# A long convolution by two-stage DFT: the second stage and its inverse as 32x32 products, and the exchanged rows from TensorE in place of DMA copies

## The chip, the cores and the metric

The kernel runs on one NeuronCore of a Trainium2 chip. The metric is device time in microseconds (us) of one execution, the median over several runs. A profile of one execution is at hand beside it. Engine names are those of the profile: PE is TensorE (PEld its weight loads), DVE is VectorE, ACT is ScalarE, POOL is GpSimd and SP is SyncE, which here only issues DMAs.

## The reference, cut to what matters

Two branches start from the same normalized input and meet at the end. Branch A is a long convolution (sequence 2048, 640 channels), done in the reference by an FFT of length 4096. Branch B is a feed-forward block with 1728 hidden units.

```python
xn = layernorm(A_q)                                   # 2048 x 640
k_shift = 4-tap causal filter of A_k with A_shift_k
kv = k_shift * A_v
y = irfft(rfft(kv, 4096) * rfft(A_ssm_k, 4096))[:2048] + kv * A_ssm_D
s = xn * y
h = gelu(xn @ B_w1 + B_b1)                            # 2048 x 1728
g = silu(h @ B_w2 + B_b2)                             # 2048 x 640
out = A_q + s * g
```

## The kernel before, in words

**The convolution.** The sequence index is split as 16 p + n, with p on the 128 partitions and n from 0 to 15. The first DFT stage is, for each n, two 128x128 products (cosine and sine matrices `WA`, `WB`), each on 640 columns in two halves of 320: `k_f1` (steps kf) for the filter, `u_f1` (uf) for the signal. Their results go through DRAM scratch (`scrK`, `scrU`) and come back with rows regrouped, so that one group g (there are 32) has on its 128 partitions 4 blocks of 32 rows: 16 values of n times real and imaginary part. The second stage is a 16-point complex DFT inside each block of 32 rows. Before the change it is one product with the 128x128 matrix `F2m`, which is zero outside its four diagonal 32x32 blocks (the mask in `small_phase`, lines 285 to 288, makes these zeros): `k_f2` (ff, line 480) for the filter, whose 32 results are kept in `Khat`, and `u_f2` (mu, line 521) for the signal. Both call `mm2` (line 335), which makes two matmuls of 128x128 by 320 columns.

**Product and inverse.** Real and imaginary parts stand on even and odd partitions, so the complex product needs the filter's rows once as they are and once with neighbours exchanged. `swap_load` (mk, line 515) fetches the exchanged rows of two groups with two DMAs on the SP queue, from `Khat` to a ring of eight slots behind it (`NR`). `product` (mp, line 523) is one VectorE instruction per group: the PSUM tile `mu` (128 x 640, f32) is read twice, times the plain and the exchanged rows, into `p` (2 x 640 columns, bf16). `inv1` (mc, line 530) is the inverse of the second stage: for each half of the columns a product with `I1a` on the first part of p and one with `I1b` on the second, accumulated in PSUM; `inv1_out` (me) evacuates it on ScalarE (three times on VectorE), and `c_store` writes it to DRAM scratch `scrC`, from which the last stage (`inv2`, steps y) reads.

**The feed-forward block** runs through the same TensorE queue: `ffn1` (h: 5 matmuls of 512 columns), its GELU on ScalarE, `ffn2` (g: 14 matmuls of 320 columns), SiLU and products.

**Order of the work.** It is written out by hand: `PLAN` is a list of step names, issued in this order; every engine runs its own instructions in the order of the list. In PLAN, a letter behind a dot says which engine evacuates (a: ScalarE, d: VectorE).

**PSUM.** The steps ff, uf, kf, mu, mc, y and some transposes take their tile from one pool, `ps_big`, of three buffers of two banks each, in turn. A step that takes a buffer waits until the tile taken three places before has been read: a mu tile by its mp, an mc tile by its me, an ff tile by its fe. A stretch of PLAN before the change:

```
mu3 mp3 mk5 ml12 h30 he30 ml11 mc2 me2.a mu4 mp4 mc1 me1.a ms0 mu5 mp5 mk6 h31 he31 ml6 ff20 fe20.a mc3 me3.a
ms1 ln15 mu6 mp6 mc4 me4.a mu7 mp7 mk7 ml9 h32 he32 mu8 mp8 mc5 me5.a ms2 mc6 me6.a mu11 mp11 mc7 me7.a ms3 mu10
```

Of the kernel before, what the change touches and what calls it, by code (L numbers as in the profile page):

```python
# [35 lines left out]
te9.a kt4 gm5 kf7 cv26 cv27 cv28 kf6 kc4.a ke6.a ke7.a ks3 g6 ge6 kf8 ke8.a kf9 ke9.d ks4 kf10 ke10.a K2 tt8
te8.a kt6 kc6.d kf11 ke11.a ks5 kt9 kc9.d gm3 kf12 ke12.a tt5 te5.d tt6 te6.a uf1 kt7 kf13 kc7.a ke13.a ks6 g7
ge7 ls12 uf0 ue0.a ue1.d us0 cv29 cv30 cv31 V3 h14 he14 kf14 ke14.d kf15 ke15.d ks7 h15 he15 kt8 kc8.d kf19 kf18
ke18.a ke19.d ks9 kt10 kc10.a cv32 cv33 cv34 cv35 cv36 kf16 ke16.a kt12 cv40 kf17 kc12.a ke17.a ks8 h16 he16 uf3
uf2 ue2.a ue3.a us1 h17 he17 kf21 kf20 ke20.a ke21.d ks10 kt11 kc11.a h18 he18 uf5 uf4 ue4.a ue5.d us2 kf22  # L40
ke22.d ls10 h19 he19 kt14 kf24 ke24.d sm kf23 kc14.a ke23.a ks11 h20 he20 kf25 ke25.d ks12 kt13 kc13.d kf28
ke28.a h21 he21 uf6 ue6.a kf29 ke29.a ks14 uf7 ue7.a us3 h22 he22 h23 he23 kf26 ke26.a gm7 cv37 cv38 cv41 cv42
cv39 kf27 ke27.a ks13 kt15 kc15.d kf30 ke30.a kf31 ke31.a ks15 fl0 fl1 fl2 h24 he24 fl4 uf10 ue10.a gm6 ls15 ls8
ls9 uf8 ue8.a ls14 uf11 ue11.a us5 h25 he25 h26 he26 uf14 ue14.a cv43 ls13 lv3 lr3 h27 he27 cv44 ls11 lv2 lr2
cv45 cv46 cv47 uf12 ue12.a uf9 ue9.a us4 fl3 uf15 ue15.a us7 g8 ge8 gm8 ln13 ln9 uf13 ue13.a us6 fl5 g9 ge9 ff3
fe3.a ln12 ff1 fe1.d ln10 ff2 fe2.a cv56 ff0 fe0.a cv48 cv49 cv50 ln8 uf21 uf20 ue20.a ue21.a us10 ff8 fe8.a
ln11 g10 ge10 uf16 ue16.a ff6 fe6.d gm9 ff9 fe9.a fl7 ff5 fe5.a ff7 fe7.a fl9 ff4 fe4.a fl8 uf17 ue17.a us8 g11
ge11 cv51 cv52 cv53 cv54 cv55 ff11 fe11.a ff10 fe10.a fl6 uf18 ue18.d uf19 ue19.a us9 fl11 uf26 ue26.a cv57 cv58
cv59 uf24 ue24.a uf27 ue27.a us13 uf25 ue25.a us12 fl12 ff16 fe16.d ff17 fe17.a fl15 ff12 fe12.a tt12 te12.a
ff14 fe14.a cv60 cv61 cv62 cv63 ff18 fe18.a ff15 fe15.a fl13 g12 ff19 fe19.a fl10 uf22 ue22.d ff13 fe13.a fl14  # L50
uf31 gm11 ge12 uf30 ue30.a ue31.d us15 ff23 fe23.d gm12 uf23 ue23.a us11 gm10 tt14 te14.d uf29 uf28 ue28.d
ue29.a us14 mk0 ml0 ml1 mk1 mk2 mk3 ml2 ml3 ml5 ml4 ff31 fe31.a tt13 te13.a tt10 te10.d it0 ie0.d ff27 fe27.d
ff25 fe25.d g13 ge13 gm13 g14 ge14 gm14 ff29 fe29.d ln14 ff28 fe28.a ff24 fe24.d g15 ge15 gm15 ff21 fe21.a tt11
te11.d ff22 fe22.a mu0 mp0 ff26 fe26.a ml7 h28 he28 mu2 mp2 ml10 ml8 mu1 mp1 mk4 mc0 me0.a h29 he29 ff30 fe30.a
mu3 mp3 mk5 ml12 h30 he30 ml11 mc2 me2.a mu4 mp4 mc1 me1.a ms0 mu5 mp5 mk6 h31 he31 ml6 ff20 fe20.a mc3 me3.a
ms1 ln15 mu6 mp6 mc4 me4.a mu7 mp7 mk7 ml9 h32 he32 mu8 mp8 mc5 me5.a ms2 mc6 me6.a mu11 mp11 mc7 me7.a ms3 mu10
mp10 h33 he33 mu9 mp9 mk8 mk9 mc8 me8.a mc10 me10.a mu12 mp12 mu13 mp13 mk10 mc11 me11.a ms5 ml14 h34 he34 ml15
mc12 me12.a it1 ie1.d mc13 me13.a ms6 mu15 mp15 h35 he35 mu14 mp14 mk11 ml13 mc9 me9.a ms4 mu18 mp18 h36 he36
mc14 me14.a mu17 mp17 h37 he37 mu16 mp16 mk12 mc15 me15.a mu20 mp20 h38 he38 mu19 mp19 mk13 mc18 me18.a h39 he39
mu21 mp21 mk14 mc16 me16.a tt17 mc19 me19.a ms9 mc17 me17.a ms8 mu23 mp23 mc20 me20.a mu22 mp22 mk15 h40 he40  # L60
# [5 lines left out]
yt5 yl8 y4 yt4 yo4 yo5 ys2 y1 yt1 yo1 ys0 y3 yt3 h47 he47 h48 he48 h49 he49 h50 he50 h51 he51 y2 yt2 yl7 yl14
yl9 yl10 yl12 yo2 yo3 ys1 q2 h52 he52 h53 he53 h54 he54 h55 he55 y6 yt6 yl13 yo6 y7 yt7 yo7 ys3 q3 y8 yt8 yo8
y11 yt11 g24 ge24 g25 ge25 g26 y12 yt12 gm24 ge26 gm25 ga24 ga25 gs25 y15 yt15 g27 ge27 y14 yt14 y13 yt13 gm26
ga26 gm27 ga27 gs27 y9 yt9 yo9 ys4 y10 yt10 yo10 yo11 ys5 g28 ge28 gm28 ga28 g29 ge29 gm29 ga29 g30 ge30 gm30
ga30 gs30 g31 ge31 gm31 ga31 gs29 gs31  # L70
"""


# [1 line left out]
def kernel(  # L75
# [170 lines left out]
    sm = {}  # L246
# [49 lines left out]
                             bias=sin_bias[:])  # L296

    def small_mats():
        nc.vector.tensor_tensor(out=mats[:], in0=sm["sn"], in1=sm["mask"], op=ALU.mult)
# [35 lines left out]
    def mm2(ps, lhsT, rhs, start=True, stop=True):  # L335
        for h in range(2):
            nc.tensor.matmul(out=ps[:, h, 0:HALF], lhsT=lhsT, rhs=rhs[:, h * HALF:(h + 1) * HALF], start=start, stop=stop)  # L337
# [182 lines left out]
    def u_f2(g):  # L520
        mm2(big_of(("mu", g)), F2m, live["uin", g // 2][:, g % 2, :])

    def product(g):
# [2 lines left out]
        nc.vector.tensor_tensor(out=p[:].rearrange("p k (h c) -> p k h c", h=2),  # L526
                                in0=live["mu", g][:, None, :, 0:HALF].to_broadcast([P, 2, 2, HALF]),
                                in1=Khat[:, g:swap + 1:swap - g, :].rearrange("p k (h c) -> p k h c", h=2), op=ALU.mult)

    def inv1(g):  # L530
        p, psC = live["p", g], big_of(("mc", g))
        for h in range(2):
# [1 line left out]
            nc.tensor.matmul(out=psC[:, h, 0:HALF], lhsT=I1a, rhs=p[:, 0, hs], start=True, stop=False)  # L534
            nc.tensor.matmul(out=psC[:, h, 0:HALF], lhsT=I1b, rhs=p[:, 1, hs], start=False, stop=True)  # L535
# [171 lines left out]
```

## Time and profile before

| | |
|---|---|
| runs | 229.04, 229.06, 227.22 us; median 229.04 |
| span of the profiled execution, first to last instruction | 225.2 us |
| the runs' times above that span | 2.0 to 3.9 us (the profiled execution's own time is not listed apart from the three) |
| granted TensorE clock, mean | 1.000 |
| DMA | 57.61 MB in 25209 packets |

Lines of the profile name an instruction's line in the kernel, its engine, what it writes and reads by tile name (output to the left of the arrow), the shapes, and its count. A timeline row has start and length in us; where several instructions are merged, the length reaches from the first one's start to the last one's end. Matmul ends are modelled, so a matmul's listed duration holds the time through the array; what successive matmuls cost is the distance of their starts. Groups list busy time and the mean of one in ns, then the idle time of the engine before them with what ended it.

### The profile page before, as it was taken

The numbers are of one execution on the slowest core, as the hardware profiler recorded it, in microseconds if no ns is written. First come the engines' busy times: TensorE is split into PE (matmuls) and PEld (weight loads), VectorE is DVE, ScalarE is ACT, GpSimd is POOL, SyncE is SP. The second block draws the span as 40 slices with busy tenths as digits, with TensorE's granted clock in tenths as the row PEclk, the third lists the DMA queues.
The fourth block names the chain that finished last, engine by engine and source line by source line (L and its number), as shares of the span: only waits on it lengthen the run. The fifth ranks groups of instructions, "written<-read, shape, count | busy, mean of one in ns | idle before, by whom it ended". The sixth has DMA issues, their size and how long they took to land.

```text
span 225.2 us, 3912 instructions
## 1 busy us (share of the span) xinstructions
PE 209.3 (93%) x1420; PEld 131.5 (58%) x1420; DVE 183.2 (81%) x309; ACT 149.7 (66%) x232; POOL 42.5 (19%) x72
## 2 busy tenths in 40 slices
PE   7869989899999899979999988999999999999993
PEld 4624457677555556645765544565777755457771
DVE  7799999989989999999859998999996125445792
ACT  3946697998988999999549665576762263671111
POOL 8000011032232345030200221203222000100010
PEclk9999999999999999999999999999999999999999
DMA  6999996645844469599849999866833694389223
GB/s 215 347 381 357 406 410 277 218 193 198 303 186 189 178 209 388 185 320 324 320 167 286 335 399 361 273 231 254 273 118 140 215 367 153 119 260 388 80 92 116
DMA packets 25209, 57.61 MB, mean 256 GB/s; under 512 B 2854, under 2 KB 14055, under 8 KB 25190
## 3 DMA queue, kind: packets, MB, share of 16 engines
q1 hardware_dynamic: 20726, 39.66, 50.7%
q0 software_dynamic: 4320, 17.70, 20.6%
q8 instruction: 11, 0.18, 0.3%
q14 instruction: 8, 0.07, 0.1%
q10 hardware_dynamic: 144, 0.01, 0.0%
HBM read 33.76 MB, written 18.35 MB: 231 GB/s over the span
## 4 chain that ended last, share of the span: by engine, by line
PE 59%; issue 13%; ACT 11%; DVE 7%; DMA 7%; SPq 1%; POOL 1%; DVEq 0%; POOLq 0%; ACTq 0%
PE g L396 20%; PE h L377 20%; ACT Khat L135 5%; DMA prm<-in_B_b_dram 4%; PE uf L337 3%; PE mc L534 2%; DMA scrC<-c 2%; PE mc L535 2%; PE kf L337 2%; PE mu L337 2%; PE y L553 2%; PE y L554 2%; DVE p L526 2%; DVE Khat L136 2%; PE ff L337 1%
## 5 line engine op out<-in xcount | busy, mean ns | idle before, releaser
L377 PE MATMUL h<-xnT,w_sb 128*128 128x512 bf16 x280 | 65.8, 379 | 1.3 <-ACT hT L383 1.0
L396 PE MATMUL g<-w_sb,hT 128*128 128x320 bf16 x448 | 63.7, 299 | 0.6 <-ACT sl L401 0.6
L396 PEld LDWEIGHTS <-hT 128*128 128x128 bf16 x448 | 43.8, 98 | 18.1 <-issue 0.8
L383 ACT ACTIVATE hT<-h,b_f 128x512 bf16<-128x512 f32 (+1 forms) x56 | 38.3, 690 | 23.2 <-PE h L377 20.7
L526 DVE TENSOR_TENSOR p<-mu,Khat 128x1280 bf16<-128x1280 f32 x32 | 45.8, 1484 | 3.1 <-PE mu L337 2.1
L377 PEld LDWEIGHTS <-w_sb 128*128 128x128 bf16 x280 | 27.3, 98 | 29.3 <-issue 1.5
L401 ACT ACTIVATE sl<-g 128x320 bf16<-128x320 f32 x32 | 14.0, 439 | 36.1 <-PE g L396 32.5
L135 ACT CAST c<-mc 128x640 bf16<-128x640 f32 x29 | 19.9, 692 | 6.5 <-PE mc L535 5.7
L541 POOL DMA_DIRECT2D scrC<-c x16 | 11.5, 718 | 51.9 <-ACT c L135 47.7
L406 DVE TENSOR_TENSOR xn<-xn,sl 128x320 bf16<-128x320 bf16 x32 | 10.0, 320 | 13.7 <-ACT sl L401 13.5
L469 DVE TENSOR_TENSOR uc<-uc,kvtmp 128x1280 bf16<-128x1280 bf16 x24 | 19.8, 824 | 0.7
L473 DVE TENSOR_TENSOR kvtmp<-kh,w_exp 128x1280 bf16<-128x1280 bf16 x24 | 19.7, 819 | 0.5
L534 PE MATMUL mc<-p,mats 128*128 128x320 bf16 x64 | 18.1, 298 | 1.6 <-DVE p L526 1.1
L560 DVE TENSOR_TENSOR t<-y,xn 128x640 bf16<-128x640 f32 x12 | 9.8, 820 | 10.6 <-PE y L554 10.5
L337 PEld LDWEIGHTS <-mats 128*128 128x128 bf16 x128 | 12.0, 97 | 10.8 <-issue 3.8
L535 PE MATMUL mc<-p,mats 128*128 128x320 bf16 x64 | 18.1, 298 | 0.0
L135 ACT CAST Khat<-uf 128x640 bf16<-128x640 f32 x26 | 17.0, 697 | 0.4 <-PE uf L337 0.4
L135 ACT CAST Khat<-ff 128x640 bf16<-128x640 f32 x24 | 15.5, 699 | 0.5 <-PE ff L337 0.4
L135 ACT CAST Khat<-kf 128x640 bf16<-128x640 f32 x22 | 15.1, 711 | 0.3 <-PE kf L337 0.2
L437 POOL DMA_DIRECT2D scrK<-Khat x16 | 8.9, 554 | 29.7 <-ACT Khat L135 16.6
L337 PE MATMUL mu<-kh,mats 128*128 128x320 bf16 x64 | 13.6, 298 | 0.8 <-DMA kh<-scrU 0.4
L337 PE MATMUL ff<-kin,mats 128*128 128x320 bf16 x64 | 12.3, 298 | 1.3 <-ACT Khat L135 1.3
(111 smaller groups left out, 269.0 us busy)
## 6 DMA issues: line engine op xcount, KB each, us to landing
scrK<-Khat POOLq DMA_DIRECT2D x16, 320.0 KB, 2.5
scrU<-Khat POOLq DMA_DIRECT2D x16, 320.0 KB, 4.3
kin<-scrK SPq DMA_DIRECT2D x16, 320.0 KB, 4.9
Khat<-Khat SPq DMA_DIRECT2D x32, 160.0 KB, 3.8
kh<-scrU SPq DMA_DIRECT2D x16, 320.0 KB, 5.2
scrC<-c POOLq DMA_DIRECT2D x16, 320.0 KB, 3.6
kh<-scrC SPq DMA_DIRECT2D x16, 320.0 KB, 6.0
kh<-in_A_k_dram SPq DMA_DIRECT2D x4, 640.0 KB, 5.9
```

The source lines that it names most:

```text
L135: return nc.scalar.copy(out=out_ap, in_=in_ap)
L337: nc.tensor.matmul(out=ps[:, h, 0:HALF], lhsT=lhsT, rhs=rhs[:, h * HALF:(h + 1) * HALF], start=start, stop=stop)
L377: nc.tensor.matmul(out=ps[:, :], lhsT=w1_sb[:, t, ft * P:(ft + 1) * P], rhs=xnT[:, t, :], start=(t == 0), stop=(t == DT - 1))
L383: nc.scalar.activation(out=hT[0:M, ft, :], in_=live["h", i][0:M, :], func=ACT.Gelu_apprx_tanh, bias=b1_f[0:M, ft:ft + 1], scale=1.0)
L396: nc.tensor.matmul(out=ps[:, 0:HALF], lhsT=hT[0:M, ft, q * P:(q + 1) * P], rhs=w2_sb[0:M, ft, hs], start=(ft == 0), stop=(ft == FT - 1))
L401: nc.scalar.activation(out=sl[:], in_=live["g", i][:, 0:HALF], func=ACT.Silu)
L469: nc.vector.tensor_tensor(out=uc[:], in0=uc[:], in1=kvtmp[:], op=ALU.add)
L473: nc.vector.tensor_tensor(out=(kvtmp if s else uc)[:], in0=kh[:, r0:r0 + KC, :], in1=w_exp[:, j:j + 1, :].to_broadcast([P, KC, D]), op=ALU ...
L526: nc.vector.tensor_tensor(out=p[:].rearrange("p k (h c) -> p k h c", h=2), in0=live["mu", g][:, None, :, 0:HALF].to_broadcast([P, 2, 2, HA ...
L534: nc.tensor.matmul(out=psC[:, h, 0:HALF], lhsT=I1a, rhs=p[:, 0, hs], start=True, stop=False)
L535: nc.tensor.matmul(out=psC[:, h, 0:HALF], lhsT=I1b, rhs=p[:, 1, hs], start=False, stop=True)
L541: nc.gpsimd.dma_start(out=pair_view(scrC)[g2], in_=live["c", g2][:])
```

## The change

The matrices become `mats` with four entries: F2, I1A, I1B, and a new F2X, which is F2 with neighbouring output columns exchanged (two small VectorE copies in `small_mats`). A product with a block-diagonal matrix is now four products of 32 rows by 32 columns on 320 columns of data. Block i of the rows goes to block (i + turn) mod 4 of the output partitions, where turn is 2g + h for group g and half h; the inverse reads these places and puts the blocks back. All tiles between the second stage and its inverse are thus in rotated order, Khat's too.

`u_f2` now makes a plain and an exchanged result in PSUM: two tiles of the pool `ps_big` (one for each half of the columns) in place of one. The exchanged rows of the filter are no longer needed, so `swap_load` and its DMAs go. `product` is two instructions per group, one for each half, each reading one PSUM tile (2 x 320) and one half of a Khat row set, read twice. PLAN is the same list without the mk steps, and with two mp steps (2g and 2g + 1) in the place of each one.

```diff
-    mats = consts.tile([P, 3, P], BF16, name="mats")
-    F2m, I1a, I1b = (mats[:, i, :] for i in range(3))
+    mats = consts.tile([P, 4, P], BF16, name="mats")
+    F2, I1A, I1B, F2X = range(4)
+    QB = 32
...
     def small_mats():
-        nc.vector.tensor_tensor(out=mats[:], in0=sm["sn"], in1=sm["mask"], op=ALU.mult)
+        nc.vector.tensor_tensor(out=mats[:, 0:3, :], in0=sm["sn"], in1=sm["mask"], op=ALU.mult)
+        for c in range(2):
+            nc.vector.tensor_copy(out=mats[:, F2X, c::2], in_=mats[:, F2, 1 - c::2])
...
+    def blocks(out, m, rhs, turn, start=True, stop=True):
+        for i in range(P // QB):
+            j = (i + turn) % (P // QB)
+            a, b = (slice(x * QB, (x + 1) * QB) for x in ((i, j) if m in (F2, F2X) else (j, i)))
+            nc.tensor.matmul(out=out[b, :], lhsT=mats[a, m, a], rhs=rhs[a, :], start=start, stop=stop)
+
+    def half(h):
+        return slice(h * HALF, (h + 1) * HALF)
...
     def k_f2(g):
-        mm2(big_of(("ff", g)), F2m, live["kin", g // 2][:, g % 2, :])
+        ps = big_of(("ff", g))
+        for h in range(2):
+            blocks(ps[:, h, 0:HALF], F2, live["kin", g // 2][:, g % 2, half(h)], 2 * g + h)
...
-    def swap_load(g2):
-        ks = take(("ks", g2), pools["ring"], None, None, "ks")
-        for a in range(2):
-            nc.sync.dma_start(out=ks[a:P:2, :, :], in_=Khat[1 - a:P:2, 2 * g2:2 * g2 + 2, :])
-
     def u_f2(g):
-        mm2(big_of(("mu", g)), F2m, live["uin", g // 2][:, g % 2, :])
-
-    def product(g):
+        ps = [big_of(("mu", 2 * g + h)) for h in range(2)]
+        for x, m in enumerate((F2, F2X)):
+            for h in range(2):
+                blocks(ps[h][:, x, 0:HALF], m, live["uin", g // 2][:, g % 2, half(h)], 2 * g + h)
+
+    def product(i):
+        g, h = divmod(i, 2)
         p = pair_of(("p", g))
-        swap = NG + g % NR
-        nc.vector.tensor_tensor(out=p[:].rearrange("p k (h c) -> p k h c", h=2),
-                                in0=live["mu", g][:, None, :, 0:HALF].to_broadcast([P, 2, 2, HALF]),
-                                in1=Khat[:, g:swap + 1:swap - g, :].rearrange("p k (h c) -> p k h c", h=2), op=ALU.mult)
+        nc.vector.tensor_tensor(out=p[:, :, half(h)], in0=live["mu", i][:, :, 0:HALF],
+                                in1=Khat[:, g:g + 1, half(h)].to_broadcast([P, 2, HALF]), op=ALU.mult)
 
     def inv1(g):
         p, psC = live["p", g], big_of(("mc", g))
-        for h in range(2):
-            hs = slice(h * HALF, (h + 1) * HALF)
-            nc.tensor.matmul(out=psC[:, h, 0:HALF], lhsT=I1a, rhs=p[:, 0, hs], start=True, stop=False)
-            nc.tensor.matmul(out=psC[:, h, 0:HALF], lhsT=I1b, rhs=p[:, 1, hs], start=False, stop=True)
+        for x, m in enumerate((I1A, I1B)):
+            for h in range(2):
+                blocks(psC[:, h, 0:HALF], m, p[:, x, half(h)], 2 * g + h, x == 0, x == 1)
```

The stretch of PLAN shown above becomes:

```
mu3 mp6 mp7 ml12 h30 he30 ml11 mc2 me2.a mu4 mp8 mp9 mc1 me1.a ms0 mu5 mp10 mp11 h31 he31 ml6 ff20 fe20.a mc3 me3.a
ms1 ln15 mu6 mp12 mp13 mc4 me4.a mu7 mp14 mp15 ml9 h32 he32 mu8 mp16 mp17 mc5 me5.a ms2 mc6 me6.a mu11 mp22 mp23 mc7 me7.a
```

More of the change, by code (lines that the diff above doesn't have):

```diff
@@ L36 @@
[L36 to L60, printed above, removed]
@@ L66 @@
[L66 to L70, printed above, removed]
+em K0 sp s A0 h0 h1 P2 ee.a A1 P1 P0 pt pb he0 he1 h2 he2 h3 he3 h4 he4 h5 he5 h6 he6 h7 he7 h8 he8 h9 he9 h10 he10
@@ new lines @@
+h11 he11 h12 he12 h13 he13 K3 ss cv8 cv0 B w cv1 cv2 cv3 cv4 cv5 cv6 cv9 cv10 cv11 cv12 cv13 cv14 K1 cv16 X1 ls4 ls5
+ls7 ls6 lv1 C0 X3 cv17 cv18 g0 ge0 gm0 g1 ge1 gm1 ws0 cv19 g2 ge2 g3 ge3 g4 cv20 cv21 cv22 ws1 g5 lr1 ln7 ln5 ws2 C4
+C3 C1 V0 cv7 cv15 C2 d kt0 kc0.a kt1 kc1.a kf0 kf1 ke0.a kt2 kc2.a V1 ln4 kf2 ke2.a cv24 cv23 X2 cv25 ke1.d ks0 gm2
+ge4 ln6 kf3 ke3.d ks1 kf4 ke4.a gm4 ge5 kt3 kc3.d kf5 ke5.a ks2 V2 tt7 te7.a kt5 kc5.d tt9 te9.a kt4 gm5 kf7 cv26 cv27
+cv28 kf6 kc4.a ke6.a ke7.a ks3 g6 ge6 kf8 ke8.a kf9 ke9.d ks4 kf10 ke10.a K2 tt8 te8.a kt6 kc6.d kf11 ke11.a ks5 kt9
@@ new lines @@
+kc9.d gm3 kf12 ke12.a tt5 te5.d tt6 te6.a uf1 kt7 kf13 kc7.a ke13.a ks6 g7 ge7 ls12 uf0 ue0.a ue1.d us0 cv29 cv30 cv31
+V3 h14 he14 kf14 ke14.d kf15 ke15.d ks7 h15 he15 kt8 kc8.d kf19 kf18 ke18.a ke19.d ks9 kt10 kc10.a cv32 cv33 cv34 cv35
+cv36 kf16 ke16.a kt12 cv40 kf17 kc12.a ke17.a ks8 h16 he16 uf3 uf2 ue2.a ue3.a us1 h17 he17 kf21 kf20 ke20.a ke21.d
+ks10 kt11 kc11.a h18 he18 uf5 uf4 ue4.a ue5.d us2 kf22 ke22.d ls10 h19 he19 kt14 kf24 ke24.d sm kf23 kc14.a ke23.a
+ks11 h20 he20 kf25 ke25.d ks12 kt13 kc13.d kf28 ke28.a h21 he21 uf6 ue6.a kf29 ke29.a ks14 uf7 ue7.a us3 h22 he22 h23
@@ new lines @@
+he23 kf26 ke26.a gm7 cv37 cv38 cv41 cv42 cv39 kf27 ke27.a ks13 kt15 kc15.d kf30 ke30.a kf31 ke31.a ks15 fl0 fl1 fl2
+h24 he24 fl4 uf10 ue10.a gm6 ls15 ls8 ls9 uf8 ue8.a ls14 uf11 ue11.a us5 h25 he25 h26 he26 uf14 ue14.a cv43 ls13 lv3
+lr3 h27 he27 cv44 ls11 lv2 lr2 cv45 cv46 cv47 uf12 ue12.a uf9 ue9.a us4 fl3 uf15 ue15.a us7 g8 ge8 gm8 ln13 ln9 uf13
+ue13.a us6 fl5 g9 ge9 ff3 fe3.a ln12 ff1 fe1.d ln10 ff2 fe2.a cv56 ff0 fe0.a cv48 cv49 cv50 ln8 uf21 uf20 ue20.a
+ue21.a us10 ff8 fe8.a ln11 g10 ge10 uf16 ue16.a ff6 fe6.d gm9 ff9 fe9.a fl7 ff5 fe5.a ff7 fe7.a fl9 ff4 fe4.a fl8 uf17
@@ new lines @@
+ue17.a us8 g11 ge11 cv51 cv52 cv53 cv54 cv55 ff11 fe11.a ff10 fe10.a fl6 uf18 ue18.d uf19 ue19.a us9 fl11 uf26 ue26.a
+cv57 cv58 cv59 uf24 ue24.a uf27 ue27.a us13 uf25 ue25.a us12 fl12 ff16 fe16.d ff17 fe17.a fl15 ff12 fe12.a tt12 te12.a
+ff14 fe14.a cv60 cv61 cv62 cv63 ff18 fe18.a ff15 fe15.a fl13 g12 ff19 fe19.a fl10 uf22 ue22.d ff13 fe13.a fl14 uf31
+gm11 ge12 uf30 ue30.a ue31.d us15 ff23 fe23.d gm12 uf23 ue23.a us11 gm10 tt14 te14.d uf29 uf28 ue28.d ue29.a us14 ml0
+ml1 ml2 ml3 ml5 ml4 ff31 fe31.a tt13 te13.a tt10 te10.d it0 ie0.d ff27 fe27.d ff25 fe25.d g13 ge13 gm13 g14 ge14 gm14
@@ new lines @@
+ff29 fe29.d ln14 ff28 fe28.a ff24 fe24.d g15 ge15 gm15 ff21 fe21.a tt11 te11.d ff22 fe22.a mu0 mp0 mp1 ff26 fe26.a ml7
+h28 he28 mu2 mp4 mp5 ml10 ml8 mu1 mp2 mp3 mc0 me0.a h29 he29 ff30 fe30.a mu3 mp6 mp7 ml12 h30 he30 ml11 mc2 me2.a mu4
+mp8 mp9 mc1 me1.a ms0 mu5 mp10 mp11 h31 he31 ml6 ff20 fe20.a mc3 me3.a ms1 ln15 mu6 mp12 mp13 mc4 me4.a mu7 mp14 mp15
+ml9 h32 he32 mu8 mp16 mp17 mc5 me5.a ms2 mc6 me6.a mu11 mp22 mp23 mc7 me7.a ms3 mu10 mp20 mp21 h33 he33 mu9 mp18 mp19
+mc8 me8.a mc10 me10.a mu12 mp24 mp25 mu13 mp26 mp27 mc11 me11.a ms5 ml14 h34 he34 ml15 mc12 me12.a it1 ie1.d mc13
@@ new lines @@
+me13.a ms6 mu15 mp30 mp31 h35 he35 mu14 mp28 mp29 ml13 mc9 me9.a ms4 mu18 mp36 mp37 h36 he36 mc14 me14.a mu17 mp34
+mp35 h37 he37 mu16 mp32 mp33 mc15 me15.a mu20 mp40 mp41 h38 he38 mu19 mp38 mp39 mc18 me18.a h39 he39 mu21 mp42 mp43
+mc16 me16.a tt17 mc19 me19.a ms9 mc17 me17.a ms8 mu23 mp46 mp47 mc20 me20.a mu22 mp44 mp45 h40 he40 mc21 me21.a ms10
+mu24 mp48 mp49 mu25 mp50 mp51 mc22 me22.a h41 he41 te17.d mc24 me24.a mu26 mp52 mp53 mc25 me25.a ms12 tt15 te15.a mu27
+mp54 mp55 tt16 te16.d mc23 me23.a ms11 mc26 me26.a tt18 te18.d mu29 mp58 mp59 it3 ie3.a mu28 mp56 mp57 g16 ge16 gm16
@@ new lines @@
+mc27 me27.a ms13 it2 ie2.d tt19 te19.a mu31 mp62 mp63 mu30 mp60 mp61 ms7 q0 g17 ge17 gm17 mc28 me28.a mc31 mc29 me29.d
+ms14 mc30 me30.d me31.d ms15 yl5 yl2 yl0 yl4 yl3 yl1 yl6 yl11 yl15 q1 g18 ge18 gm18 g19 ge19 gm19 g20 ge20 gm20 g21
+ge21 gm21 g22 ge22 gm22 g23 ge23 gm23 h42 he42 h43 he43 y0 yt0 yo0 h44 he44 h45 he45 h46 he46 y5 yt5 yl8 y4 yt4 yo4
+yo5 ys2 y1 yt1 yo1 ys0 y3 yt3 h47 he47 h48 he48 h49 he49 h50 he50 h51 he51 y2 yt2 yl7 yl14 yl9 yl10 yl12 yo2 yo3 ys1
+q2 h52 he52 h53 he53 h54 he54 h55 he55 y6 yt6 yl13 yo6 y7 yt7 yo7 ys3 q3 y8 yt8 yo8 y11 yt11 g24 ge24 g25 ge25 g26 y12
@@ L71 @@
+yt12 gm24 ge26 gm25 ga24 ga25 gs25 y15 yt15 g27 ge27 y14 yt14 y13 yt13 gm26 ga26 gm27 ga27 gs27 y9 yt9 yo9 ys4 y10
+yt10 yo10 yo11 ys5 g28 ge28 gm28 ga28 g29 ge29 gm29 ga29 g30 ge30 gm30 ga30 gs30 g31 ge31 gm31 ga31 gs29 gs31
 """
@@ L668 @@
         "fl": kin_load, "ff": k_f2, "fe": k_f2_out, "it": i2_tr, "ie": i2_out,
-        "ml": uin_load, "mk": swap_load, "mu": u_f2, "mp": product, "mc": inv1, "me": inv1_out, "ms": c_store,
+        "ml": uin_load, "mu": u_f2, "mp": product, "mc": inv1, "me": inv1_out, "ms": c_store,
         "q": xq_load, "yl": cab_load, "y": inv2, "yt": gate, "yo": out_add, "ys": out_store,
```

10 lines of the change are left out of this document (removed).

## The prediction

> **What bounds the kernel now.** I read the busy shares and the chain of waits first.
>
> ```profile
> span 225.2 us, 3912 instructions
> PE 209.3 (93%) x1420; PEld 131.5 (58%) x1420; DVE 183.2 (81%) x309; ACT 149.7 (66%) x232; POOL 42.5 (19%) x72
> PE 59%; issue 13%; ACT 11%; DVE 7%; DMA 7%; SPq 1%; POOL 1%; DVEq 0%; POOLq 0%; ACTq 0%
> ```
>
> TensorE is busy 93% of the span and carries most of the chain. But shares average over stages, so next comes the table by stretches, cut where the changed steps run: ff from 85 us, mu and mc from 117.5 to 171 us, then the rest.
>
> ```profile
> core 0: us, PE busy (x) PEld busy (x) DVE busy (x) ACT busy (x) POOL busy (x), PEclk, DMA share, GB/s
> 85.00:117.50 32.50, 29.82 (x217) 19.68 (x215) 28.89 (x49) 25.16 (x44) 6.68 (x12) 1.00 0.81 279
> 117.50:171.00 53.50, 51.14 (x342) 31.38 (x343) 49.67 (x43) 36.88 (x55) 10.04 (x14) 1.00 0.79 278
> 171.00:225.20 54.20, 50.38 (x330) 31.94 (x327) 26.35 (x53) 18.20 (x30) 4.71 (x8) 1.00 0.55 195
> ```
>
> The middle stretch has two engines at their limit: PE 51.1 and DVE 49.7 of 53.5 us. DVE does the products here:
>
> ```profile
> L526 DVE TENSOR_TENSOR p<-mu,Khat 128x1280 bf16<-128x1280 f32 x32 | 45.8, 1484 | 3.1 <-PE mu L337 2.1 <-DMA Khat<-Khat 0.8
> L526 DVE TENSOR_TENSOR p<-mu,Khat x32: 1477/1481/1492, 118.0 to 168.1; 128x1280 bf16<-128x1280 f32 x32
> 119.73 7.12 DVE L526 TENSOR_TENSOR p<-mu,Khat 128x1280 bf16<-128x1280 f32 x5 [0.26 <-DMA Khat<-Khat]
> ```
>
> From the first product's start to the last one's end are 168.1 + 1.48 - 118.0 = 51.6 us. In a run of five the starts are (7.12 - 1.48)/4 = 1.41 us apart. DVE waited 2.1 us for mu and 0.8 us for exchanged rows: the DMAs that go were nearly hidden, and nearly all they can give is 0.8 us.
>
> **What PE does in that stretch** (same stretch, grouped), and starts in a row:
>
> ```profile
> L534 PE MATMUL mc<-p,mats 128*128 128x320 bf16 x64 | 18.1, 298 | 1.6 <-DVE p L526 1.1 <-ACT c L135 0.2
> L535 PE MATMUL mc<-p,mats 128*128 128x320 bf16 x64 | 18.1, 298 | 0.0
> L377 PE MATMUL h<-xnT,w_sb 128*128 128x512 bf16 x70 | 17.4, 379 | 0.0
> L337 PE MATMUL mu<-kh,mats 128*128 128x320 bf16 x64 | 13.6, 298 | 0.8 <-DMA kh<-scrU 0.4 <-DVE p L526 0.2 <-ACT c L135 0.2
> L396 PE MATMUL g<-w_sb,hT 128*128 128x320 bf16 x28 | 4.3, 299 | 0.0
> L368 PE MATMUL tt<-ident,xn 128*128 128x128 bf16 x20 | 1.9, 219 | 0.0
> L337 PE MATMUL ff<-kin,mats 128*128 128x320 bf16 x6 | 1.3, 298 | 0.0
> L488 PE MATMUL it<-ident,WB 128*128 128x128 bf16 x16 | 1.2, 219 | 0.0
> L488 PE MATMUL it<-ident,WA 128*128 128x128 bf16 x8 | 0.6, 219 | 0.0
> L396 PE MATMUL g<-w_sb,hT 65*128 65x320 bf16 x2 | 0.6, 301 | 0.0
> 120.23 1.24 PE L377 MATMUL h<-xnT,w_sb 128*128 128x512 bf16 x5
> 166.66 2.07 PE L396 MATMUL g<-w_sb,hT 128*128 128x320 bf16 x14
> 165.44 0.61 PE L488 MATMUL it<-ident,WB 128*128 128x128 bf16 x8
> ```
>
> Distances of starts: 320 columns (2.07 - 0.30)/13 = 0.136 us; 512 columns (1.24 - 0.38)/4 = 0.215; transposes (0.61 - 0.22)/7 = 0.056. PE's work here without mu, mc and ff is 70 x 0.215 + 30 x 0.136 + 44 x 0.056 = 21.6 us; mu, mc and ff are 198 x 0.136 = 26.9.
>
> **The change: matmuls.** mu goes from 2 to 16 matmuls per group, mc from 4 to 16, ff from 2 to 8: 1280 in place of 256, each with its own weight load, still 320 columns long. Everything hangs on the price of one such pair, which this trace does not show. Nearest rows: the 0.136 above, and the shortest matmuls in the kernel, ten of 64 columns with a weight load each:
>
> ```profile
> L305 PE MATMUL psw<-ident,skp x40: 219/348/348, 3.9 to 11.0; 128*128 128x64 bf16 x40
> 10.53 0.72 PE L305 MATMUL psw<-ident,skp 128*128 128x64 bf16 x10
> ```
>
> These lie (0.72 - 0.22)/9 = 0.056 us apart, though 64 columns stream in a fifth of the 0.136 that 320 take. If the four row parts work at once and nothing else limits, a pair costs 0.136/4 = 0.034; if the parts of both halves do (eight places are in use within a group), 0.136/8 = 0.017; all sixteen, 0.0085; if load and issue limit, 0.056; if the parts run in turn, 0.136. I take 0.034: four products then do what one masked product did, in the same time, and it lies between the nearest rows' 0.056 and 0.017.
>
> The Trainium skill, page "TensorE: Matmul & The Clock Gate", Part 3 on packing small matmuls, reports that sixteen 32x32 products started about 4 ns apart and ran 10.6 times faster than in turn. By it a pair would be an estimated 0.136/10.6 = 0.013 us, near my second case; no run here shows it yet.
>
> **Changes of shape.** Whatever a change between 128- and 32-row matmuls costs, if the array must first empty it is at most 0.298 - 0.136 = 0.16 us. In PLAN, ff, mu and mc stand in 37 unbroken runs, 24 of them with mu or mc: up to 48 x 0.16 = 7.7 us in the middle stretch and 26 x 0.16 = 4.2 before it; nothing if they overlap. I take half. The Trainium skill, "TensorEngine Tiling (Array Packing)", Tiling Modes, Key Properties, says that changing the mode drains the engine; by it the sum takes the full figures, some 6 us more.
>
> **Products and PSUM.** A product becomes two of 128x640 f32. Rows of that size:
>
> ```profile
> L560 DVE TENSOR_TENSOR t<-y,xn x12: 815/817/825, 185.1 to 216.5; 128x640 bf16<-128x640 f32 x12
> 170.39 2.29 DVE L136 CAST c<-mc 128x640 bf16<-128x640 f32 x3 [0.58 <-PE mc L535]
> ```
>
> One lasts 0.82; in a row they lie (2.29 - 0.82)/2 = 0.735 apart. A pair costs 1.47 when the next follows at once, 0.735 + 0.82 = 1.555 when DVE must stop. And now it must stop. mu takes two of three PSUM buffers, mc the third: mu4 gets its buffers from mp6 and mp7, the two halves of mu3, so PE cannot finish mu4 while DVE still reads mu3. Before, a mu took one buffer, and DVE never paused for it. Going through PLAN, 22 of the 31 handovers hang on the last product (all but mu1, 8, 9, 13, 14, 16, 19, 25, 30). The two signals of a handover:
>
> ```profile
> 138.91 1.48 DVE L526 TENSOR_TENSOR p<-mu,Khat 128x1280 bf16<-128x1280 f32 x1
> 140.44 0.30 PE L534 MATMUL mc<-p,mats 128*128 128x320 bf16 x1 [0.23 <-DVE p L526]
> 126.90 0.43 PE L337 MATMUL mu<-kh,mats 128*128 128x320 bf16 x2
> 127.36 1.49 DVE L526 TENSOR_TENSOR p<-mu,Khat 128x1280 bf16<-128x1280 f32 x1 [0.17 <-PE mu L337]
> ```
>
> DVE to PE 0.05, PE to DVE 0.03. Between them PE must issue what is left up to the first half's exchanged product: 8 pairs where only the second buffer waits (13 times), 12 where the first does (9 times), on average 8.6 steps, plus 0.30 through the array. The gap is 0.38 + 8.6 p: 0.67 us at p = 0.034.
>
> DVE's chain: 22 x 1.555 + 10 x 1.47 = 48.9; 22 x 0.67 = 14.7; its other work (49.7 - 45.8 = 3.9), half of it in gaps, 2. That is 65.6 against 51.6: +14.0. PE alone needs 21.6 + (1024 + 24) x 0.034 = 57.2, with half the shape changes 61, so neither hides in the other: where an h (5 x 0.215 = 1.08) stands beside an mc (16 x 0.034 = 0.54), PE comes 0.06 to 0.39 later than DVE's 1.555 (14 times), beside the two g 1.0 to 1.3: between 2.9 and 8.1, middle 5.5. Middle stretch: +19.5.
>
> **The rest.** The 29 ff groups before it cost 8 x 0.034 against 2 x 0.136, the same; shape changes +2. The two copies in small_mats are each smaller than this row, I take 0.2 each:
>
> ```profile
> L299 DVE TENSOR_TENSOR mats<-Khat,GA x1: 549/549/549, 69.2 to 69.2; 128x384 bf16<-128x384 f32 x1
> ```
>
> SP issues 32 DMAs fewer, which lets the uin loads queued behind them start sooner; mu waited 0.4 us for those, which I leave at nothing. After 171 us nothing changes; it only starts later. Sum: 19.5 + 2 + 0.4 = +22; span 247; the runs lie 2.0 to 3.9 above the span: 250.
>
> **Rivals.** *Eight parts at once, p = 0.017.* The gap is 0.53, the chain 48.9 + 11.6 + 2 = 62.5 (+10.9), PE late by some 2.5; ff saves at most 29 x 0.136 = 3.9, of which ACT's and DVE's share in that stretch (25.2 and 28.9 of 32.5 busy) leaves part, less its shape changes: -1. In all +13: 242. For it: the turn sends the halves to different columns of the array.
> *Loads and issue bound, p = 0.056.* PE in the middle stretch: 21.6 + 1048 x 0.056 + 3.8 = 84 against 53.5, +30.5; ff 29 x (0.45 - 0.27) = +5 and 2; 267, with full shape changes 273. For it: the psw rows.
> *The change doesn't do what it says:* the parts run one after another. 1280 x 0.136 - 256 x 0.136 = +139: 368. For it speaks only that no row shows two matmuls streaming at once.
> *Faster:* half products cheaper than their size says. If they cost what bf16 sources cost,
>
> ```profile
> L564 DVE TENSOR_TENSOR w_exp<-t,xq x12: 484/492/493, 185.9 to 217.7; 128x640 bf16<-128x640 bf16 x12
> ```
>
> 64 x 0.49 = 31, and with eight parts at once 31 + 11.6 + 2 = 45 against 51.6; with ff's 1 some 8 us less: 221. It decides from 0.59 us a half (51.6 - 13.6 over 64). Against it: one source stays f32 in PSUM, as in the L560 rows at 0.82.
>
> **Chances.** Forecast 0.40, eight parts 0.27, load bound 0.20, in turn 0.05, faster 0.05, and 0.03 that handovers hide and it comes out even, within 1% (2.3 us, about what can be told here). All but the last two are slower: 0.92. The range takes in the second and third case with their unknown shape changes: 236 to 276.
>
> **What would show it.** The span from first to last product (66 to 73 us forecast, 51.6 before); waits of DVE's products for mu, about 22 near 0.5 to 0.7 us, where all of them came to 2.1 us before; half products at 0.82; pairs of a group 0.034 apart; no Khat DMAs. PE without holes in the middle stretch would mean load bound; PE holes with short bursts, eight parts at once. I am wrong at the root if DVE runs its halves back to back: then the PSUM count is wrong.

## The result, and the profile after

| | before | after |
|---|---|---|
| median of the runs | 228.13 us (4 runs, 226.75 to 229.06) | 245.25 us (4 runs, 243.93 to 246.83) |
| ratio | | 1.077 (95% interval 1.068 to 1.085) |
| span of the profiled execution | 225.2 us | 244.3 us |
| first product's start to last product's end | 51.6 us | 67.7 us |

The change makes the kernel slower by 7.7%. The forecast was 250 (236 to 276), slower with a chance of 0.92. A ratio leaves out runs that lie more than 1.5% above the fastest of their kernel, so it can differ from the quotient of two medians. The page of the changed kernel begins with the span and the busy shares:

```profile
span 244.3 us, 5920 instructions
PE 212.3 (87%) x2425; PEld 120.1 (49%) x2444; DVE 187.5 (77%) x343; ACT 150.0 (61%) x232; POOL 42.3 (17%) x72
```

PE's share fell from 93% to 87%. Its busy time hardly moved, but that is no measure of its work, since in short bursts each matmul's way through the array is counted in full. The VectorE products, as groups and with their first and last start, show where the time went:

```profile
L536 DVE TENSOR_TENSOR p<-mu,Khat 128x640 bf16<-128x640 f32 x64 | 49.4, 819 | 12.1 <-PE mu L344 9.4 <-ACT c L133 1.1 <-issue 0.7
L536 DVE TENSOR_TENSOR p<-mu,Khat x64: 811/816/826, 120.1 to 187.0; 128x640 bf16<-128x640 f32 x64
```

The stretch of the products runs from 120.1 to 187.0 + 0.8, 67.7 us, 16.1 more than before, out of 19.1 more in the span. The same two stretches by engine, first the kernel before, then the changed one:

```profile
118.00:169.60 51.60, 49.24 (x330) 30.03 (x329) 48.47 (x40) 35.94 (x54) 10.04 (x14) 1.00 0.80 282
```

```profile
120.10:187.80 67.70, 52.83 (x1098) 22.16 (x1109) 52.28 (x71) 35.31 (x51) 10.02 (x14) 0.97 0.44 146
```

DVE (the third busy time) worked 52.3 - 48.5 = 3.8 us more, and stood idle 67.7 - 52.3 = 15.4 us where it had been idle 3.1. That is the whole 16.1. DMA share fell from 0.80 to 0.44: the copies are gone, and with them only the 0.8 us that products had waited for exchanged rows. Of the 12.1 us that DVE stood ahead of products, 0.6 lie ahead of the first one, outside the stretch, and 11.5 inside. The other 4.0 us are waits of other VectorE work that stands in PLAN behind PE's late transposes and g. The two longest, in the stretch of the products:

```profile
L134 DVE COPY GA<-it 128x1024 bf16<-128x1024 bf16 x1 | 0.7, 690 | 2.8 <-PE it L500 2.8
L416 DVE TENSOR_TENSOR xn<-xn,sl 128x320 bf16<-128x320 bf16 x1 | 0.3, 325 | 1.0 <-ACT sl L411 1.0
```

In the same stretch of the kernel before, the first of these waits does not appear, and the second is 0.2:

```profile
L136 DVE COPY GA<-it 128x1024 bf16<-128x1024 bf16 x1 | 0.7, 681 | 0.0
L406 DVE TENSOR_TENSOR xn<-xn,sl 128x320 bf16<-128x320 bf16 x2 | 0.6, 320 | 0.2 <-ACT sl L401 0.2
```

The remaining 3 us of the span: the products begin 2.1 us later, and 0.9 more follow behind them. The late start is no work of the change. A kernel below that is the kernel before up to 171 us (shape_changes) starts them at 119.6, with the granted clock below full in the same two early slices of the page as here (the third and the fourth):

```profile
PEclk9988999999999999999999997999999999999999
```

```profile
PEclk9988999999999999999999999999999999999998
```

The first is the changed kernel, the second shape_changes; before, all slices read 9. The other traces agree: the six whose early slices all read 9 start their first product between 117.9 and 118.8, the eight with the early drop between 119.6 and 121.8. So some 17 of the 19.1 us between the two spans belong to the change, as much as between the two medians.

**A handover, seen in the timeline** of the changed kernel:

```profile
157.81 2.48 DVE L536 TENSOR_TENSOR p<-mu,Khat 128x640 bf16<-128x640 f32 x3
160.35 0.44 PE L344 MATMUL mu<-kh,mats 32*32 32x320 bf16 x10 [0.41 <-DVE p L536]
160.74 2.50 DVE L536 TENSOR_TENSOR p<-mu,Khat 128x640 bf16<-128x640 f32 x3 [0.45 <-PE mu L344]
```

DVE ends its product at 160.29; only then does PE get the second buffer, starts at 160.35, and DVE goes on at 160.74. Both have stood: PE 0.41, DVE 0.45 us.

**What a small matmul costs.** Four rows of the changed kernel, of 16 weight loads and matmuls each for mu and mc, and of ff:

```profile
135.91 0.46 PE L344 MATMUL mu<-kh,mats 32*32 32x320 bf16 x16
136.35 0.46 PE L344 MATMUL mc<-p,mats 32*32 32x320 bf16 x16
106.43 0.33 PE L344 MATMUL ff<-kin,mats 32*32 32x320 bf16 x8
98.16 0.35 PE L344 MATMUL ff<-kin,mats 32*32 32x320 bf16 x16
```

One matmul is listed at 0.30. So 8 start within 0.03 us, and the 16 of two ff groups, whose four turns take all sixteen places, within 0.05: 3 to 4 ns from one to the next. The 16 of one mu or mc use eight places twice and take one more streaming time (0.46 - 0.30 = 0.16). Per pair that is 0.136/8 = 0.017 us in a mu or mc.

### The profile page after: what moved, and what is told of

It reads as the page before. It is cut to its first block, busy times and chain, and to the rows that moved or that the text cites. A ratio compares the mean times of both kernels' runs of the same rounds, so it can differ in the third digit from the quotient of the medians.

```text
span 244.3 us, 5920 instructions
## 1 busy us (share of the span) xinstructions
PE 212.3 (87%) x2425; PEld 120.1 (49%) x2444; DVE 187.5 (77%) x343; ACT 150.0 (61%) x232; POOL 42.3 (17%) x72
## 5 line engine op out<-in xcount | busy, mean ns | idle before, releaser
L393 ACT ACTIVATE hT<-h,b_f 128x512 bf16<-128x512 f32 (+1 forms) x56 | 38.3, 690 | 34.8 <-PE h L387 32.1
L536 DVE TENSOR_TENSOR p<-mu,Khat 128x640 bf16<-128x640 f32 x64 | 49.4, 819 | 12.1 <-PE mu L344 9.4
L406 PEld LDWEIGHTS <-hT 128*128 128x128 bf16 x448 | 43.2, 98 | 19.2 <-issue 2.1
L387 PEld LDWEIGHTS <-w_sb 128*128 128x128 bf16 x280 | 26.7, 100 | 33.6 <-issue 8.1
L344 PEld LDWEIGHTS <-mats 32*32 32x32 bf16 x1280 | 15.0, 88 | 41.9 <-issue 39.2
L344 PE MATMUL mu<-kh,mats 32*32 32x320 bf16 x512 | 20.1, 299 | 9.1 <-DVE p L536 7.1
L344 PE MATMUL mc<-p,mats 32*32 32x320 bf16 x512 | 15.1, 307 | 4.6 <-DVE p L536 2.5
L568 DVE TENSOR_TENSOR t<-y,xn 128x640 bf16<-128x640 f32 x12 | 9.8, 820 | 10.6 <-PE y L562 10.5
L457 POOL DMA_DIRECT2D scrU<-Khat x16 | 8.8, 553 | 23.9 <-ACT Khat L133 23.8
L576 POOL DMA_DIRECT2D out_dram<-w_exp x6 | 3.3, 544 | 42.4 <-DVE w_exp L572 41.0
```

Source lines behind the costliest of these rows:

```text
L344: nc.tensor.matmul(out=out[b, :], lhsT=mats[a, m, a], rhs=rhs[a, :], start=start, stop=stop)
L387: nc.tensor.matmul(out=ps[:, :], lhsT=w1_sb[:, t, ft * P:(ft + 1) * P], rhs=xnT[:, t, :], start=(t == 0), stop=(t == DT - 1))
L393: nc.scalar.activation(out=hT[0:M, ft, :], in_=live["h", i][0:M, :], func=ACT.Gelu_apprx_tanh, bias=b1_f[0:M, ft:ft + 1], scale=1.0)
L406: nc.tensor.matmul(out=ps[:, 0:HALF], lhsT=hT[0:M, ft, q * P:(q + 1) * P], rhs=w2_sb[0:M, ft, hs], start=(ft == 0), stop=(ft == FT - 1))
L536: nc.vector.tensor_tensor(out=p[:, :, half(h)], in0=live["mu", i][:, :, 0:HALF], in1=Khat[:, g:g + 1, half(h)].to_broadcast([P, 2, HALF]), ...
L568: nc.vector.tensor_tensor(out=halves(o), in0=live["y", n2][:, :, 0:HALF], in1=halves(xr), op=ALU.mult)
```

## The experiments

Theory H says that DVE and PE take turns because a mu holds two of three PSUM buffers. Its rivals: S, the shape changes and the many small matmuls hold DVE up; E, the blocks or the exchange on PE are the cost; and the split of the product in itself. Ratios are against the kernel before, run on the same chip.

### one_tile_dma_swap: the blocks alone

```diff
 # the kernel before, with blocks() for ff, mu and mc
     def u_f2(g):
-        mm2(big_of(("mu", g)), F2m, live["uin", g // 2][:, g % 2, :])
+        ps = big_of(("mu", g))
+        for h in range(2):
+            blocks(ps[:, h, 0:HALF], F2, live["uin", g // 2][:, g % 2, half(h)], 2 * g + h)
```

> The kernel before with nothing changed but the 32x32 products (ff, mu and mc in blocks; one PSUM tile per mu, one product instruction, exchanged rows by DMA as before). Theory H (DVE and PE take turns because a mu needs two of three PSUM buffers): the turns are gone, so DVE goes back to one product each 1.41 us, the stretch from first to last product to 51 to 53 us, and the time to 226 to 230. Theory S (the shape changes and the many small matmuls on PE hold DVE up): these are all still here but for the exchanged products, so the stretch stays above 58 us and the time above 234.

Measured: 229.98 us, ratio 1.005 (1.001 to 1.010). The group of the products, with waits almost as before (46.0/32 = 1.44 us each), and by engine its own stretch from the first product to the last, which takes 52.7 us:

```profile
L540 DVE TENSOR_TENSOR p<-mu,Khat 128x1280 bf16<-128x1280 f32 x32 | 46.0, 1485 | 3.8 <-PE mu L344 2.1 <-DMA Khat<-Khat 0.8 <-PE h L387 0.6
120.50:173.20 52.70, 42.39 (x883) 19.41 (x887) 48.77 (x40) 35.41 (x54) 10.01 (x14) 0.97 0.80 279
```

H holds; S is out. The second row is as telling: PE is busy 42.4 us of 52.7 where it had been 49.2 of 51.6, and the kernel is no faster, since DVE still needs 49.

### one_tile_no_exchange: the split, without the second tile

```diff
 # the changed kernel
-        ps = [big_of(("mu", 2 * g + h)) for h in range(2)]
-        for x, m in enumerate((F2, F2X)):
-            for h in range(2):
-                blocks(ps[h][:, x, 0:HALF], m, live["uin", g // 2][:, g % 2, half(h)], 2 * g + h)
+        ps = big_of(("mu", g))
+        for h in range(2):
+            blocks(ps[:, h, 0:HALF], F2, live["uin", g // 2][:, g % 2, half(h)], 2 * g + h)
...
-        nc.vector.tensor_tensor(out=p[:, :, half(h)], in0=live["mu", i][:, :, 0:HALF],
+        nc.vector.tensor_tensor(out=p[:, :, half(h)], in0=live["mu", g][:, h:h + 1, 0:HALF].to_broadcast([P, 2, HALF]),
```

> The changed kernel without the exchanged product: mu is one PSUM tile with both halves, each half product reads its half of it twice. The exchange of neighbouring rows is left out. Blocks, shape changes and the two half products stay. H: no turns, DVE bound by 64 half products at 0.735 us in a row, 47 us and its other work 4, stretch 51 to 54, time 227 to 232. S: eight of 32 small matmuls fewer per group and the same shape changes, above 238. If the split of the product is what costs, it stays near 245 less nothing.

Measured: 226.59 us, ratio 0.996 (0.992 to 0.999), just under the range expected.

```profile
L535 DVE TENSOR_TENSOR p<-mu,Khat 128x640 bf16<-128x640 f32 x64 | 47.5, 815 | 1.6 <-PE mu L344 1.4
```

The half products follow each other 47.5/64 = 0.74 us apart and wait 1.6 us in all. This kernel leaves out the exchange of neighbouring rows. It has every shape change of the changed one, no DMA copies and the split product; without the second tile and the exchanged matmuls the loss is gone.

### two_tiles_alone: the second tile and the split, without anything else

```diff
 # the kernel before
-        mm2(big_of(("mu", g)), F2m, live["uin", g // 2][:, g % 2, :])
+        ps = [big_of(("mu", 2 * g + h)) for h in range(2)]
+        for h in (1, 0):
+            nc.tensor.matmul(out=ps[h][:, 0, 0:HALF], lhsT=F2m, rhs=live["uin", g // 2][:, g % 2, h * HALF:(h + 1) * HALF],
+                             start=True, stop=True)
...
-        nc.vector.tensor_tensor(out=p[:].rearrange("p k (h c) -> p k h c", h=2),
-                                in0=live["mu", g][:, None, :, 0:HALF].to_broadcast([P, 2, 2, HALF]),
-                                in1=Khat[:, g:swap + 1:swap - g, :].rearrange("p k (h c) -> p k h c", h=2), op=ALU.mult)
+        for h in range(2):
+            hs = slice(h * HALF, (h + 1) * HALF)
+            nc.vector.tensor_tensor(out=p[:, :, hs], in0=live["mu", 2 * g + h][:, 0:1, 0:HALF].to_broadcast([P, 2, HALF]),
+                                    in1=Khat[:, g:swap + 1:swap - g, hs], op=ALU.mult)
```

> The kernel before (128x128 products, exchange by DMA) with only this changed: a mu takes two PSUM tiles, one for each half, and the product is two instructions, one for each; the second half's matmul is issued first, so that the first product stands behind the wait for both. PE streams as much as before, no change of shape. H (the turns over PSUM): about 22 handovers of 0.5 to 0.65 us and 3 us for the split, 240 to 247. Theory E (the blocks or the exchange on PE are the cost): 228 to 231.

Measured: 243.81 us, ratio 1.067 (1.057 to 1.077).

```profile
L531 DVE TENSOR_TENSOR p<-mu,Khat 128x640 bf16<-128x640 f32 x64 | 48.9, 818 | 11.9 <-PE mu L523 9.6 <-ACT c L135 1.0 <-DMA scrC<-c 0.8
```

With 128x128 products, with the DMA copies, with no more matmuls than before, the waits are the same 11.9 us. Taking the second buffer, with the split that goes with it, brings 6.7% of the 7.7%, and the intervals overlap; E is out as the main cause, and what is left for it is the one point between.

### split_alone

The kernel before with the product in two halves as in the last diff, but both out of one tile: `in0=live["mu", g][:, h:h + 1, 0:HALF]`.

> The kernel before with the product in two halves, out of one PSUM tile as before. H: only the split's own price, 64 x 0.735 against 32 x 1.41 = +2 us, 229 to 231. If the split is what breaks the overlap of DVE and PE, 235 or more.

Measured: 229.59 us, ratio 1.006 (1.001 to 1.011). The split alone costs 1.3 us (0.1 to 2.5 by the interval).

### full_array_exchange: the changed kernel without 32x32 products

```diff
     def blocks(out, m, rhs, turn, start=True, stop=True):
-        for i in range(P // QB):
-            ...
+        nc.tensor.matmul(out=out, lhsT=mats[:, m, :], rhs=rhs, start=start, stop=stop)
```

> The changed kernel, but with 128x128 products in place of the blocks (F2, F2X, I1A, I1B as whole masked matrices, no rotation): no change of shape on PE, the two PSUM tiles and the two half products stay. H: a handover still costs about 0.05 + 0.136 + 0.30 + 0.03 = 0.5 us, and PE has 13 us more to stream in the stretch, so 243 to 252. S: without shape changes most of the loss is gone, 228 to 236.

Measured: 248.74 us, ratio 1.092 (1.085 to 1.098). Slower than the changed kernel: S would have had most of the loss go. DVE waited 14.9 us ahead of products instead of 12.1, which fits a handover with whole matmuls of 0.136 us in it:

```profile
L533 DVE TENSOR_TENSOR p<-mu,Khat 128x640 bf16<-128x640 f32 x64 | 49.4, 819 | 14.9 <-PE mu L341 11.3 <-issue 1.1 <-ACT xnT L133 0.8
```

So within the changed kernel the 32x32 products win some 3 us back, though the two intervals touch.

### half_first and halves_apart: easing the turns

half_first exchanges the two loops of `u_f2`:

```diff
-        for x, m in enumerate((F2, F2X)):
-            for h in range(2):
+        for h in range(2):
+            for x, m in enumerate((F2, F2X)):
                 blocks(ps[h][:, x, 0:HALF], m, live["uin", g // 2][:, g % 2, half(h)], 2 * g + h)
```

> The changed kernel with the two loops of u_f2 exchanged: plain and exchanged rows of the first half, then those of the second. H: where only the second tile waits (13 of the 22 handovers) the first half is ready before DVE is done, and DVE's wait of some 0.45 us goes; the other 9 keep it. DVE's waits ahead of products fall from 12.1 to about 6 us and the time from 245 to 238 to 241. S: PE's work and its shape changes are the same, 245 as before.

Measured: 242.03 us, ratio 1.063 (1.056 to 1.071); waits 10.5 us, not 6: a miss, with about a quarter of the expected fall. Its interval overlaps that of the changed kernel (1.068 to 1.085), so alone it decides little between H and S. The expectation of the next run gives a reason for the miss, which is argued and not measured. Then halves_apart makes the halves two steps (ma, mb), with the mc that stood ahead of a mu between them:

```diff
-mc2 me2.a mu4 mp8 mp9 mc1 me1.a ms0 mu5 mp10 mp11
+ma4 mp8 mc2 me2.a mb4 mp9 ma5 mp10 mc1 me1.a ms0 mb5 mp11
```

> The changed kernel with u_f2 as two steps, one for each half and its PSUM tile, and in PLAN the mc that stood ahead of a mu moved between its halves; all computations stay. In half_first PE stood at the second half's wait with an mc and an h behind it, so what one turn gained the next one lost. H, with that: the second half's wait now lies behind an mc, DVE's waits ahead of products fall from 12.1 us to 5 to 8, the time from 245 to 236 to 240. If it is not PE's place in the list but the count of buffers alone, no change against half_first: 241 to 243.

Measured: 240.16 us, ratio 1.049 (1.042 to 1.055), just above what H expected, and waits of 8.9 us, also above it:

```profile
L504 DVE TENSOR_TENSOR p<-mu,Khat 128x640 bf16<-128x640 f32 x64 | 48.7, 817 | 8.9 <-PE mu L307 4.6 <-PE mc L307 3.1 <-ACT c L96 0.6
```

Both steps go the way of H. The second has the same three buffers, and its interval lies just below that of half_first and clear of the changed kernel's: PE's place in its own list counts beside the count of buffers. No run gives `ps_big` a fourth buffer, which would be the most direct trial of H. What is left of the waits is behind mu and mc (4.6 and 3.1 us); why each of these is late was not followed up.

### shape_changes: the price of going from 128 to 32 rows and back

```diff
 # the kernel before, ffn2, in the loop over ft
+            if i >= 18 and ft in (4, 9):
+                nc.tensor.matmul(out=ps[0:32, 0:HALF], lhsT=mats[0:32, 0, 32:64], rhs=w2_sb[0:32, ft, hs], start=False, stop=False)
```

> The kernel before with 28 more matmuls of 32x32 by 320 columns, each between two 128x128 ones, two in each of the last 14 g, where PE is the bound; they add zeros from an empty block of mats. By the starts in the changed kernel's trace (0.231 us from a 128-row start to a 32-row one, 0.237 back, against 0.136 within one shape) each adds 0.33: +9.3 us, 236 to 238. If a change costs nothing in itself, 28 x 0.136 = +3.8, 231 to 232.

Measured: 238.16 us, ratio 1.040 (1.031 to 1.050), which is 9.2 us of 228.25, or 0.33 for each of the 28 (0.25 to 0.41 by the interval). In the timeline:

```profile
180.78 0.57 PE L396 MATMUL g<-w_sb,hT 128*128 128x320 bf16 x3
181.28 0.30 PE L399 MATMUL g<-w_sb,mats 32*32 32x320 bf16 x1
181.51 0.85 PE L396 MATMUL g<-w_sb,hT 128*128 128x320 bf16 x5
```

The last of the three starts at 180.78 + 0.57 - 0.30 = 181.05, the small one 0.23 later, the next 128-row one again 0.23 later, where starts of one shape lie 0.136 apart. A change, with the weight load that goes with it, costs 0.09 to 0.10 us.

### Four attempts to use PE's free time

blocks_replanned is one_tile_dma_swap with a changed PLAN; the others cast some mu tiles on ScalarE first, so that VectorE reads bf16:

```diff
     def product(g):
         p = pair_of(("p", g))
         swap = NG + g % NR
+        if g in CAST:
+            um = row_of(("um", g))
+            cast("a", um[:], live["mu", g])
+            nc.vector.tensor_tensor(out=p[:], in0=um[:, None, :].to_broadcast([P, 2, D]),
+                                    in1=Khat[:, g:swap + 1:swap - g, :], op=ALU.mult)
+            return
```

> The kernel before with the blocks in ff, mu and mc (one tile, exchange by DMA), and PLAN changed: the h of the third chunk closer together, four g in place of two in the stretch of the products, their VectorE products two steps later, the first y behind four more h. H: PE has some 10 us free there, of which two g more use 3.8: 224 to 227. If PE's free time there can't be used, 229 or more.

> one_tile_dma_swap, and for 10 of the 32 groups ScalarE first casts the mu tile to a bf16 row in SBUF, from which VectorE makes the product. A bf16 product of 128x1280 took 0.82 us in these traces (the tap products), from PSUM 1.48; a cast takes ScalarE 0.69, which had 36 of 53.5 us busy there. If the freed PE time was worth nothing only because VectorE bounds the stretch: VectorE loses 10 x 0.66 = 6.6 us, the stretch goes from 53 to 47 to 49, the time from 230 to 224 to 227. If PE's order or waits bound it too: 228 or more.

> The kernel before with the same ten casts and nothing else. PE is busy 51.1 of 53.5 us in the stretch with 128x128 products, so there is little room: 226 to 229, 0 to 2 us under the kernel before. If VectorE alone bounded the kernel before: 221 to 223.

> As blocks_cast10 with 15 groups: VectorE 9.9 us less, about 43, ScalarE 36 + 10.4 = 47, PE 43 of 53. If the stretch goes with the busiest engine: 47 to 48 us, no better than ten casts by more than 1 us, 223 to 226.

Measured, in this order: 233.21 us, ratio 1.018 (1.008 to 1.028); 231.56, 1.015 (1.009 to 1.021); 229.44, 1.008 (1.004 to 1.012); 229.65, 1.001 (0.996 to 1.006). All lie above the range expected; the first two came out where their expectations had put them in case PE's free time can't be used (blocks_replanned), or PE's order or waits bound the stretch too (blocks_cast10). The products did become cheaper, and new waits took their place. Of blocks_cast10, the two kinds of product, and of blocks_cast15 the longest wait:

```profile
L547 DVE TENSOR_TENSOR p<-mu,Khat 128x1280 bf16<-128x1280 f32 x22 | 32.1, 1485 | 4.7 <-PE mu L345 2.0 <-DMA Khat<-Khat 2.0 <-DMA scrC<-c 0.7
L544 DVE TENSOR_TENSOR p<-um,Khat 128x1280 bf16<-128x1280 bf16 x10 | 8.2, 823 | 7.4 <-ACT um L136 4.1 <-DMA Khat<-Khat 3.0
```

```profile
DVE p L544 <- ACT um L136: 9.5, 10, 1.6
```

The products cost 32.1 + 8.2 = 40.3 us in place of 46.0, and waited 12.1 in place of 3.8, for the casts and now also 5.0 us for the exchanged rows, which had been 0.8. No kernel of these computes the whole and beats the kernel before; whether a new PLAN for the blocks would, stays open.

## Why the prediction was right, point by point

**The bound.** That the middle stretch is bound by DVE beside PE, not by PE alone as the chain's 59% would have it, holds: in one_tile_dma_swap PE's busy time in it is 6.9 us less, and the kernel is no faster.

**The turns over PSUM** were the largest term, 14.7 us, and are shown by both halves of the proof: the second tile with the split brings 6.7% (two_tiles_alone), of which the split alone has 0.6 (split_alone), and without it the loss is gone (one_tile_no_exchange). They also stand where the forecast put them. Of its 22 handovers 20 have a wait ahead of the product in the changed kernel's trace, and the other two (mu29, mu31) hide behind other VectorE work; the nine that it excepted wait 0.17 us at most. (That DVE "never paused" for a mu before was a little too strong: it had waited 2.1 us in four places.)

**Their size** is what the forecast had wrong. The 20 waits come to 10.9 us, 0.55 each, and ten of them read 0.45 or 0.46; the forecast had 22 of 0.67 and, apart from them, 5.5 us for PE coming late. In the trace such lateness is inside the 10.9, and few waits are much longer than the rest (0.70, 0.99 and 1.09).

**The price of a pair** is the term behind both. Forecast 0.034, measured 0.017 in mu and mc: the first rival's price, and in ff, where two groups take all sixteen places, less. Inside a handover it is less still, since there 8 pairs on 8 different places start within 0.03 us. The Trainium skill's 4 ns between starts ("TensorE: Matmul & The Clock Gate", Part 3) agrees with the 3 to 4 ns here. So the case that came true by its price is the first rival, with a chance of 0.27, not the forecast with its 0.40, and 245 lies nearer to the rival's 242 than to 250.

**Luck in the total.** For the stretch the forecast added 50.9 us of DVE work and 20.2 of waits, together 71.1. The trace has 52.3 of work, 11.5 of waits ahead of products, and 4.0 of other waits that neither case had, 67.7. The forecast's handovers and late PE were too large by 8.7, and what it left out gave 5.4 back. The longest of these other waits, GA's copy, seems to belong to the turns only in part. It is 2.8 us in the two kernels whose granted clock fell there (the changed kernel and half_first), and 1.2 to 1.4 in the three kernels with turns whose clock was full, as here in two_tiles_alone:

```profile
DVE GA L136 <- PE it L488: 1.4, 1, 1.4
```

**Shape changes.** Half of 0.16, so 0.08 each, was taken; 0.09 to 0.10 was measured. The Trainium skill's rule that a mode change drains the engine ("TensorEngine Tiling (Array Packing)", Tiling Modes) agrees in that each change costs time; the full 0.16 that the prediction put beside it was too much. In the changed kernel 74 of these come to an estimated 7 us of PE, which full_array_exchange shows are more than paid back by the smaller streaming time. The 2 us that they were to cost ahead of the stretch did not come: half_first has the same ff blocks, and with the early clock full its products start at 117.9, where the kernel before has 118.0:

```profile
L536 DVE TENSOR_TENSOR p<-mu,Khat x64: 814/816/826, 117.9 to 183.8; 128x640 bf16<-128x640 f32 x64
```

**The split** was put at 0.06 us a group, 1.9 in all, while products run in a row, and at 3.8 with the stops; split_alone gave 1.3, and DVE's busy time in the stretch rose by 3.8. **The DMA copies** were put at 0.8 us at most; one_tile_no_exchange, which has none, is 0.4% under the kernel before.

**The rivals.** Load and issue bound (267) and in turn (368) fell with the 3 to 4 ns between starts. The faster one needed half products under 0.59 us; they take 0.74 in a row and 0.82 alone. That handovers hide, so that it comes out even, held for two of the 22 alone.

## What to carry to other kernels

Before a cheaper product is put on an engine, look at which engine the stretch waits for, and count the buffers between the two: a producer that needs all the buffers its consumer is reading turns two engines that ran side by side into two that take turns, and the price is a signal each way plus the way through the array, some 0.45 to 0.55 us each time here. Small block products in a big array can be nearly free in streaming, but each change of shape had its own price, 0.09 to 0.10 us here, so they belong in long unbroken runs.

## What was not expected of the hardware

Small matmuls with their own weight loads started 3 to 4 ns apart (16 in 0.35 us), while the shortest full-width pairs of this kernel lie 56 ns apart. And in the traces of six of the eight kernels with blocks (not of one_tile_no_exchange and halves_apart) the granted clock fell for a few microseconds in the middle stretch or just behind it; in the six traces without blocks it did not fall there. Its cause is open. Here the changed kernel, with 0.75 and 0.82:

```profile
144.00:148.00 4.00, 2.73 (x51) 0.86 (x37) 3.02 (x4) 1.05 (x2) 0.18 (x1) 0.75 0.23 78
148.00:152.00 4.00, 3.69 (x62) 1.47 (x62) 1.36 (x2) 2.07 (x3) 0.92 (x2) 0.82 0.22 82
```
